# Four decoded weight units stay on chip through the later groups' first layers; five coded buffers instead of nine

## The chip, the core and the metric

The kernel runs on one core of a Trainium2 chip. The core has TensorE (PE, matrix products), VectorE (DVE), ScalarE (ACT), GpSimd (POOL) and SyncE (SP), which here only issues loads and stores; 16 DMA engines move the data. Every engine works through its own queue in order and waits on semaphores of the others. The metric is the device time of one execution in microseconds (us), the median of several runs.

## What is computed

Attention with 2 batches, 8 heads, 576 positions and a head size of 64, then an ELU-like layer of 512 to 2048 to 512, then a mixture of four experts of 512 to 1024 to 512, weighted by normalised probabilities:

```python
scores = scale * np.matmul(q, k.transpose(0, 1, 3, 2))
bias = -(cum[:, :, :, None] - cum[:, :, None, :])        # cum: running sum of max(s, 0)
scores = np.where(causal, -1e9, scores + np.minimum(bias, 0.0))
attn = np.exp(scores - scores.max(-1, keepdims=True))
attn = attn / (attn.sum(-1, keepdims=True) + 1e-09)
x = np.matmul(attn, v)                                   # as (1152, 512)
h = x @ w_in
g = np.where(h > 0.0, h, np.exp(np.minimum(h, 0.0)) - 1.0)
x = g @ w_out
p = domain_probs / (domain_probs.sum(-1, keepdims=True) + 1e-09)
for e in range(4):
    out += p[:, e:e + 1] * (np.maximum(x @ w1[e], 0.0) @ w2[e])
```

## The kernel before

**Tokens and units.** The 1152 tokens are worked in three groups of 256, 448 and 448. The first layer's weights are cut into 16 units (0 to 15) of 128 hidden columns with their 128 rows of w_out, 512 KB each; the experts' into 32 more (units 16 to 47). Group 0 runs its first layer (matmuls "up", L717, and "acc", L704) and then the experts (L614, as three matmuls of high and low halves). Group 1 and 2 run their first layers with L614 as well, and share the experts' layer behind that. The attention of the positions that group 0 doesn't need runs as a background to all this, one small step between two matmuls.

**Coded units.** For group 0 the 16 units come coded, two halves of 512 KB per unit, 32 halves in all, loaded by SP (L131). `decode_halves` turns a half into fp32: ACT takes the magnitude (L150) and the low bits (L157, into z), DVE puts them together (L158, L160). A decoded pair of units lies in a tile "wu" of a ring of five. When a unit is complete, POOL writes it to w_dec in DRAM (L163). In groups 1 and 2 `fetch` (L97, SP) reads each unit back from w_dec into a tile "raw" (ring of three), and `prepare` splits it into a high half (ACT, L103) and a low half (DVE, L87) in a "wu" tile. Units 16 and on are fetched by the same L97 from in_w.

**Where halves wait.** The coded halves of the first lap lie in tiles that are not needed yet: 2 in a wu tile, 3 in gt tiles, 9 in "cd" tiles made for them, then 11 in yh, yl, raw, xa and ox; the second lap takes yh, yl, raw and xa again. A half is loaded when the one that had its place is decoded.

**What the background needs.** `load_small` (L422, L424) loads the first 128 positions into a tile pt (five loads), `load` (L444 to L462) the first two larger jobs (eight loads each). `split` makes qs (L478), kh (L479), qb (L481) and kl (L87) of one head and loads 2 KB of bias rows behind qb and kl (L476, L477, from rows_d). One head's block is then: two score matmuls (L490 on kh and qs, L492 on kl and qb), DVE's reduction (L527), ACT's exponential (L532), DVE's normalisation (L505 to L507), PE's transpose (L542), ACT's copy of it (L557), and PE's product with v (L569). Scores and transposes share two banks "att". A first layer up uses one of two banks "up": PE may write one again when ACT (L721, L724) and DVE (L725) have read it.

**What sets the order.** The program names its operations in a loop over units, and a scheduler then orders each engine's queue when the kernel is built. On the chip each queue is fixed; SP may have eight loads under way.

Of the kernel before, what the change touches and what calls it, by code (L numbers as in the profile page):

```python
# [8 lines left out]
F32 = mybir.dt.float32  # L9
# [10 lines left out]
NAB, NCD = DFF // 128, F // 128  # L20
NU = NAB + E * NCD
# [26 lines left out]

N_LOW = 4

N_WU, N_GT, N_CD = 1, 3, 9

@with_exitstack
def tile_kernel(ctx, tc, qT, kT, v, s, w64, w, probs, out):
# [12 lines left out]
    psum = ctx.enter_context(tc.tile_pool(name="ps", bufs=1, space=bass.MemoryType.PSUM))  # L67
    PE, DVE, ACT, POOL, SP = nc.tensor, nc.vector, nc.scalar, nc.gpsimd, nc.sync

    BASE = ("ident", "mask", "maskp", "zero", "cum", "cum_2", "cum_t0", "cum_t1",  # L70
            "xa", "ox", "pr")
    EDGE = ("cum_p0", "cum_p1", "sm", "prs")
    L1 = ("wu", "raw", "gt", "e", "yh", "yl", "z0", "z1", "xf")

    def sb(shape, tag, bufs, dtype=F32):
        p = (base if tag in BASE else edge if tag in EDGE else l1_pool if tag in L1
             else att_pool[0])
        return p.tile(shape, dtype, tag=tag, name=tag, bufs=bufs)
# [9 lines left out]


    w64 = w64.bitcast(I32)  # L90
    w_dec = tc.dram_tile([NAB, 128, 1024], F32, name="w_dec")
    n_units = NU + NAB * (len(GROUPS) - 1)
    fetched, units = {}, {}

    def fetch(n):
        fetched[n] = t = sb([128, 1024], "raw", 3)
        SP.dma_start(out=t, in_=w[n - NAB] if n < NU else w_dec[(n - NU) % NAB])  # L97

# [8 lines left out]
    order = [(0, 0)] + [h for n in range(NAB - 1) for h in ((n + 1, 0), (n, 1))] + [(NAB - 1, 1)]  # L107

    small = [("yh", 1, 1), ("yl", 1, 1)] + [("raw", 3, 1)] * 3 + [("xa", 1, 3), ("ox", 1, 3)]
    turn = [("wu", 5, 2)] * N_WU + [("gt", 3, 1)] * N_GT + [("cd", N_CD, 1)] * N_CD + small * 2  # L110
    places = [(tag, bufs, n, i) for tag, bufs, n in turn for i in range(n)]
    coded, freed_by, last_in = {}, [], {}
    for i, (tag, bufs, many, k) in enumerate(places):
# [21 lines left out]
    def decode_halves(upto):  # L135

        while n_decoded[0] < min(upto, len(order)):  # L140
            i = n_decoded[0]
            n, part = order[i]
            if part == 0:
                if n % 2 == 0:
                    pair = sb([128, 2, 1024], "wu", 5)
                    units[n], units[n + 1] = pair[:, 0], pair[:, 1]
            x, m = coded.pop(i), units[n][:, 512 * part:512 * part + 512]
            high, low, mi = x[:, :, 1], x[:, :, 0], m.bitcast(I32)
            tc.keep_in_program_order(
                ACT.activation(m, high.bitcast(F32), AF.Abs, scale=2.0 ** -112))  # L150
            z = sb([128, 512], f"z{i % 2}", 1, I32)
            if i < N_LOW:
                tc.keep_in_program_order(DVE.tensor_scalar(
                    z, low.bitcast(U32), 7.49 / 2 ** 32, None, op0=ALU.mult))
            else:
                tc.keep_in_program_order(
                    ACT.activation(z, low.bitcast(U32), AF.Copy, scale=7.49 / 2 ** 32))  # L157
            DVE.scalar_tensor_tensor(out=mi, in0=mi, scalar=3, in1=z,  # L158
                                     op0=ALU.logical_shift_left, op1=ALU.bitwise_or)
            DVE.scalar_tensor_tensor(out=mi, in0=high, scalar=-2 ** 31, in1=mi,  # L160
                                     op0=ALU.bitwise_and, op1=ALU.bitwise_or)
            if part:
                POOL.dma_start(out=w_dec[n], in_=units[n])  # L163
            n_decoded[0] += 1
            fetch_halves()


    ident = sb([128, 128], "ident", 1)
    make_identity(nc, ident)

    mask = sb([128, S], "mask", 1)
# [3 lines left out]
    maskp = sb([128, 64], "maskp", 1)  # L175
# [6 lines left out]
    zero = sb([64, 256], "zero", 1)  # L182
# [7 lines left out]
    cum = sb([B * H, S], "cum", 1)  # L190
# [579 lines left out]
    yh, yl = (sb([128, NCC, tok], t, 1, F32R) for t in ("yh", "yl"))  # L770
# [3 lines left out]
    pr = pr_first  # L774
# [316 lines left out]
```

## Time and profile before

| | |
|---|---|
| median of 3 runs | 712.02 us (711.47 to 712.31) |
| span of the profiled execution, first to last instruction | 710.54 us (its whole time is not listed apart; the median is 1.48 above this span) |
| PE busy | 695.7 us (98%), 3670 instructions |
| DVE busy | 561.8 us (79%) |
| ACT busy | 366.9 us (52%) |
| POOL busy | 17.7 us (2%) |
| moved by DMA | 97.00 MB |
| mean granted TensorE clock | 0.997 |

The page is one profiled execution. Times are from the start of its span. A row of a timeline merges neighbouring equal instructions; "[3.94 <-DVE gt L725]" is idle time of that engine before the row, and what ended it. PE's instructions overlap, so a batch of eight that starts every 1.73 us is listed with 1.89.

### The profile page before, as it was taken

How to read it: one execution, taken by the hardware profiler on the slowest of the kernel's cores; microseconds unless marked ns; L12 is line 12 of the kernel's file. 1: busy time of each engine (PE TensorE's matmuls, PEld its weight loads, DVE VectorE, ACT ScalarE, POOL GpSimd, SP SyncE). 2: the span in 40 equal slices, each digit the busy share in tenths (PEclk: the TensorE clock that was granted, in tenths of full speed). 3: DMA queues.
4: the chain of work that ended last, by engine and by line, in shares of the span. 5: the costliest groups of instructions: out<-in, count | busy, mean ns of one | idle time of the engine just before them, and what ended most of it. 6: DMA issues, size and time to landing. Idle time of an engine off the chain costs nothing.

```text
span 710.5 us, 10311 instructions
## 1 busy us (share of the span) xinstructions
PE 695.7 (98%) x3670; PEld 594.1 (84%) x3670; DVE 561.8 (79%) x1158; ACT 366.9 (52%) x765; POOL 17.7 (2%) x40
## 2 busy tenths in 40 slices
PE   8999899999999999999999999999999999999997
PEld 7787688887878887887899988888888888888886
DVE  7798679887868988875975469988888888888765
ACT  5897679676667777666754343322222233322320
POOL 5011000000000000000000000000000000000000
PEclk9999999999999999999999999999999999999999
DMA  8999965765674553523552000111111111111002
GB/s 301 410 391 380 318 204 179 226 206 171 185 222 149 173 174 94 161 98 102 226 178 89 1 1 0 60 60 59 60 60 59 60 60 59 60 60 59 1 0 105
DMA packets 40868, 97.00 MB, mean 137 GB/s; under 512 B 4096, under 2 KB 17616, under 8 KB 40816
## 3 DMA queue, kind: packets, MB, share of 16 engines
q1 hardware_dynamic: 38288, 87.67, 37.0%
q0 software_dynamic: 2528, 8.67, 3.0%
q8 instruction: 29, 0.48, 0.3%
q14 instruction: 23, 0.19, 0.1%
HBM read 85.32 MB, written 11.01 MB: 136 GB/s over the span
## 4 chain that ended last, share of the span: by engine, by line
PE 89%; ACT 6%; DVE 2%; DMA 2%; issue 1%; POOL 0%; ACTq 0%; DVEq 0%; POOLq 0%
PE acc L614 39%; PE up L614 17%; PE att L926 11%; PE up L926 8%; PE att L569 3%; PE att L542 3%; ACT z L157 2%; ACT wu L150 2%; DMA raw<-in_w 2%; PE att L497 1%; PE att L490 1%; PE att L492 1%; PE acc L704 1%; PE att L362 1%; PE up L717 1%
## 5 line engine op out<-in xcount | busy, mean ns | idle before, releaser
L614 PE MATMUL acc<-w,h 128*128 128x512 f32 x672 | 172.0, 392 | 0.0
L614 PEld LDWEIGHTS acc<-w,h 128*128 128x128 f32 x672 | 126.1, 188 | 23.0 <-ACT h L936 0.2
L87 DVE TENSOR_TENSOR wu<-raw,wu 128x1024 fp32r<-128x1024 f32 x64 | 78.0, 1220 | 18.7 <-ACT wu L103 18.2
L614 PE MATMUL acc<-gt,wu 128*128 128x448 f32 x384 | 87.8, 372 | 0.0
L671 DVE SCALAR_TENSOR_TENSOR ox<-acc,pr,ox 128x512 f32<-128x512 f32 x105 | 78.5, 748 | 11.4 <-PE acc L614 9.1
L936 ACT ACTIVATE h<-c 128x448 fp32r<-128x448 f32 x48 | 27.4, 573 | 111.2 <-DVE c L942 111.2
L614 PEld LDWEIGHTS acc<-gt,wu 128*128 128x128 f32 x384 | 70.1, 188 | 7.8 <-issue 2.6
L103 ACT ACTIVATE wu<-raw 128x1024 fp32r<-128x1024 f32 x64 | 67.5, 1055 | 16.7 <-PE acc L614 14.5
L926 PE MATMUL att<-S,top 128*128 128x448 f32 x288 | 66.3, 365 | 0.0
L926 PEld LDWEIGHTS att<-S,top 128*128 128x128 f32 x288 | 54.0, 188 | 6.7 <-issue 0.2
L614 PE MATMUL acc<-wu,gt 128*128 128x512 f32 x192 | 56.1, 408 | 0.0
L614 PE MATMUL up<-yh,wu 128*128 128x256 f32 x256 | 53.4, 289 | 0.0
L937 DVE SCALAR_TENSOR_TENSOR h<-c,h 128x448 fp32r<-128x448 f32 x48 | 29.8, 623 | 18.7 <-ACT h L936 18.7
L614 PEld LDWEIGHTS up<-yh,wu 128*128 128x128 f32 x256 | 41.7, 189 | 3.4 <-issue 1.5
L926 PE MATMUL up<-x2a,top 128*128 128x448 f32 x192 | 44.2, 366 | 0.0
L614 PE MATMUL up<-xa,wu 128*128 128x448 f32 x192 | 43.5, 371 | 0.0
L614 PE MATMUL up<-ox,wu 128*128 128x448 f32 x192 | 41.5, 366 | 0.8 <-DVE e L729 0.8
L721 ACT ACTIVATE e<-up 128x448 f32<-128x448 f32 (+1 forms) x48 | 23.5, 489 | 34.0 <-PE up L614 30.2
L532 ACT ACTIVATE p<-p,nm 128x384 f32<-128x384 f32 (+4 forms) x56 | 34.5, 617 | 12.3 <-DVE nm L527 11.9
L926 PEld LDWEIGHTS up<-x2a,top 128*128 128x128 f32 x192 | 35.9, 188 | 4.8 <-ACT p L951 0.6
L936 ACT ACTIVATE h<-up 128x448 fp32r<-128x448 f32 x16 | 8.8, 547 | 59.5 <-PE up L926 59.5
L614 PEld LDWEIGHTS up<-ox,wu 128*128 128x128 f32 x192 | 36.0, 188 | 4.0 <-DVE e L729 1.1
(193 smaller groups left out, 1223.8 us busy)
## 6 DMA issues: line engine op xcount, KB each, us to landing
raw<-in_w SPq DMA_DIRECT2D x38, 512.0 KB
raw<-w_dec SPq DMA_DIRECT2D x32, 512.0 KB
raw<-in_w SPq DMA_DIRECT2D x16, 1024.0 KB
w_dec<-wu POOLq DMA_DIRECT2D x16, 512.0 KB, 7.4
cd<-in_w SPq DMA_DIRECT2D x9, 512.0 KB
k<-in_kT SPq DMA_DIRECT2D x16, 288.0 KB
xa<-in_w SPq DMA_DIRECT2D x5, 512.0 KB
cbp<-cum_d SPq DMA_DIRECT2D x16, 144.0 KB
```

The lines of the kernel that those rows point to most:

```text
L87: DVE.tensor_tensor(out=lo, in0=x, in1=hi.bitcast(F32), op=ALU.subtract)
L103: ACT.activation(t[:, 0], x, AF.Copy)
L150: ACT.activation(m, high.bitcast(F32), AF.Abs, scale=2.0 ** -112))
L532: ACT.activation(p, p, AF.Exp, bias=nm, scale=-1.0, accum_out=sm)
L542: PE.transpose(pt[:cb[c + 1] - cb[c], m, :], p[:, cb[c]:cb[c + 1]], ident)
L569: PE.matmul(o[64 * j:64 * j + 64, qs:nq], job["v"][:n, c, 64 * j:64 * j + 64], job["pt"][:n, j, c, qs:nq], start=c == 0, stop=c == n_c - 1)
L614: PE.matmul(o, a[m], b[n], start=first and i == 0, stop=last and i == 2)
L671: DVE.scalar_tensor_tensor(out=o_sb, in0=o, scalar=pr[:, i, e:e + 1], in1=o_sb, op0=ALU.mult, op1=ALU.add)
L721: ACT.activation(e, o, AF.Exp)
L926: PE.matmul(bank, tops[q][:, m, op, cs], x[:, n, c], start=first and c + i == 0, stop=c == 1 and i == 2, skip_group_check=True)
L936: ACT.activation(h[:, 0, u, cs], c, AF.Relu)
L937: DVE.scalar_tensor_tensor(out=h[:, 1, u, cs], in0=c, scalar=0.0, in1=h[:, 0, u, cs].bitcast(F32), op0=ALU.max, op1=ALU.subtract)
```

## The change

Two tiles "wr" of one pair of units each (16 KB per partition) are added. The decoded units 12 to 15 go into them rather than into wu, stay there until both later groups have split them, and are neither written to w_dec nor read back: 4 writes and 8 reads of 512 KB each are gone. The wr tiles hold the first four coded halves before that. The cd tiles become five instead of nine, and the tags zero, cum, cum_2, z0 and z1 move to the pool that is closed when the background begins.

```diff
-N_WU, N_GT, N_CD = 1, 3, 9
+N_WR, N_WU, N_GT, N_CD = 2, 1, 3, 5
+N_KEPT = 2 * N_WR
...
-    BASE = ("ident", "mask", "maskp", "zero", "cum", "cum_2", "cum_t0", "cum_t1",
-            "xa", "ox", "pr")
+    BASE = ("ident", "mask", "maskp", "cum_t0", "cum_t1", "xa", "ox", "pr")
     EDGE = ("cum_p0", "cum_p1", "sm", "prs")
-    L1 = ("wu", "raw", "gt", "e", "yh", "yl", "z0", "z1", "xf")
+    L1 = ("wr", "wu", "raw", "gt", "e", "yh", "yl", "xf")
...
-    w_dec = tc.dram_tile([NAB, 128, 1024], F32, name="w_dec")
+    w_dec = tc.dram_tile([NAB - N_KEPT, 128, 1024], F32, name="w_dec")
     n_units = NU + NAB * (len(GROUPS) - 1)
-    fetched, units = {}, {}
+    fetched, units, kept = {}, {}, {}
 
     def fetch(n):
+        if n >= NU and (n - NU) % NAB in kept:
+            fetched[n] = kept[(n - NU) % NAB]
+            return
...
-    turn = [("wu", 5, 2)] * N_WU + [("gt", 3, 1)] * N_GT + [("cd", N_CD, 1)] * N_CD + small * 2
+    turn = [("wr", N_WR, 2)] * N_WR + [("wu", 5, 2)] * N_WU + [("gt", 3, 1)] * N_GT + [("cd", N_CD, 1)] * N_CD + small * 2
...
                 if n % 2 == 0:
-                    pair = sb([128, 2, 1024], "wu", 5)
+                    if n < NAB - N_KEPT:
+                        pair = sb([128, 2, 1024], "wu", 5)
+                    else:
+                        pair = sb([128, 2, 1024], "wr", N_WR)
+                        kept[n], kept[n + 1] = pair[:, 0], pair[:, 1]
                     units[n], units[n + 1] = pair[:, 0], pair[:, 1]
...
-            if part:
+            if part and n not in kept:
                 POOL.dma_start(out=w_dec[n], in_=units[n])
```

The scheduler's order changes with it, in group 0, at the passage from the first layer to the experts. Lines of the changed kernel stand 3 to 7 lower: L97 becomes L100, L103 L106, L157 L164, L478 to L481 L485 to L488, L490 and L492 L497 and L499, L542 L549, L614 L621, L717 L724, L721 and L724 L728 and L731.

ACT, the decodes of the last halves (raw, xa) and the exponentials of the last units; before:

```order
L157 ACTIVATE z_760<-raw 128x512
L481 ACTIVATE qb<-pt 64x128 x2
L478 ACTIVATE qs<-pt 128x128 x2
L721 ACTIVATE e<-up 128x256
L724 ACTIVATE e<-e 128x256
L150 ACTIVATE wu<-xa 128x512
L157 ACTIVATE z_779<-xa 128x512
L150 ACTIVATE wu<-xa 128x512
L157 ACTIVATE z_785<-xa 128x512
L103 ACTIVATE wu<-raw 128x1024
L721 ACTIVATE e<-up 128x256
```

and in the changed kernel:

```order
L164 ACTIVATE z_756<-raw 128x512
L728 ACTIVATE e<-up 128x256
L731 ACTIVATE e<-e 128x256
L157 ACTIVATE wr<-xa 128x512
L164 ACTIVATE z_775<-xa 128x512
L157 ACTIVATE wr<-xa 128x512
L164 ACTIVATE z_780<-xa 128x512
L106 ACTIVATE wu<-raw 128x1024
L728 ACTIVATE e<-up 128x256
L106 ACTIVATE wu<-raw 128x1024
L731 ACTIVATE e<-e 128x256
L106 ACTIVATE wu<-raw 128x1024
```

The splits of pt (qb, qs) moved behind the exponential of unit 11 (the first e here), the decodes of xa and three splits of raw tiles, which follow one another sooner.

SP, the loads behind the last coded halves (xa<-in_w); before:

```order
L131 DMA xa<-in_w 128x1024 x2
L422 DMA pt<-in_qT 64x8x128 x2
L422 DMA pt<-in_kT 64x8x128
L97 DMA raw<-in_w 128x1024
L422 DMA pt<-in_kT 64x8x128
L97 DMA raw<-in_w 128x1024
L424 DMA pt<-in_v 128x512
```

and in the changed kernel:

```order
L134 DMA xa<-in_w 128x1024 x2
L100 DMA raw<-in_w 128x1024 x3
L429 DMA pt<-in_qT 64x8x128 x2
L429 DMA pt<-in_kT 64x8x128 x2
L431 DMA pt<-in_v 128x512
```

Three raw tiles (units 16 to 18) are fetched ahead of pt. Unit 19 follows 16 job loads and two pairs of bias rows later (before, units 18 and 19 followed the job loads directly, and two pairs of bias rows stood far ahead, before the second lap's yh).

PE, from the first expert's accumulation (acc, after 24 and 36 up matmuls) on; before:

```order
L614 MATMUL acc_1147<-wu,gt 128x512 x3
L614 MATMUL acc_1148<-wu,gt 128x512 x3
L614 MATMUL acc_1147<-wu,gt 128x512 x3
L614 MATMUL acc_1148<-wu,gt 128x512 x3
L614 MATMUL up<-yh,wu 128x256
L614 MATMUL up<-yl,wu 128x256
L614 MATMUL up<-yh,wu 128x256 x2
L614 MATMUL up<-yl,wu 128x256
L492 MATMUL att<-kl,qb 128x128
```

and in the changed kernel:

```order
L621 MATMUL acc_1141<-wu,gt 128x512 x3
L621 MATMUL acc_1142<-wu,gt 128x512 x3
L499 MATMUL att<-kl,qb 128x128
L497 MATMUL att<-kh,qs 128x128
L499 MATMUL att<-kl,qb 128x128
L549 MATMUL att<-ident,p 128x128
L497 MATMUL att<-kh,qs 128x128
L499 MATMUL att<-kl,qb 128x128
L621 MATMUL up<-yh,wu 128x256
L621 MATMUL up<-yl,wu 128x256
L499 MATMUL att<-kl,qb 128x128
L621 MATMUL up<-yh,wu 128x256 x2
```

The L492 and L542 of the first heads, which stood among the last units' matmuls of the first layer, now stand in a row behind 18 acc matmuls; of the four first L490 there, two stay. The number of instructions on PE, ACT and DVE is the same; SP has 8 fewer loads, POOL 4 fewer writes. In groups 1 and 2 the order is the same but for the splits that read wr.

## Rows read from the trace of the kernel before

**Rows 1.** The page, busy time, share of the span and instructions of each engine

```profile
PE 695.7 (98%) x3670; PEld 594.1 (84%) x3670; DVE 561.8 (79%) x1158; ACT 366.9 (52%) x765; POOL 17.7 (2%) x40
```

**Rows 2.** Windows: length, PE, PEld, DVE, ACT, POOL busy, PE clock, DMA share, GB/s

```profile
200.00:250.00 50.00, 49.82 (x299) 42.10 (x298) 39.08 (x104) 33.90 (x79) 0.00 (x0) 1.00 0.58 182
```

**Rows 3.** Instructions on w_dec: count, ns min/median/max, first and last start

```profile
L97 SPq DMA_DIRECT2D raw<-w_dec x32: 319/333/1482, 198.0 to 383.8; - x32
L163 POOL DMA_DIRECT2D w_dec<-wu x16: 532/534/571, 27.1 to 79.7; - x16
```

**Rows 4.** PE's timeline from 66 to 97 us: start, us, engine, line, tiles

```profile
66.33 1.89 PE L717 MATMUL up<-xf,wu 128*128 128x256 f32 x8
68.05 1.89 PE L704 MATMUL acc<-gt,wu 128*128 128x256 f32 x8
73.88 2.80 PE L717 MATMUL up<-xf,wu 128*128 128x256 f32 x8 [3.94 <-DVE gt L725]
...
83.14 0.41 PE L490 MATMUL att<-kh,qs 128*128 128x128 f32 x1
83.39 0.27 PE L492 MATMUL att<-kl,qb 68*128 68x128 f32 x1
...
90.83 0.47 PE L614 MATMUL up<-yh,wu 128*128 128x256 f32 x1
...
93.89 2.91 PE L614 MATMUL acc<-wu,gt 128*128 128x512 f32 x12
96.64 0.28 PE L614 MATMUL up<-yh,wu 128*128 128x256 f32 x1
```

**Rows 5.** Windows of 4 us around the end of the first layer

```profile
64.00:68.00 4.00, 4.00 (x20) 3.54 (x19) 3.81 (x8) 2.43 (x5) 0.53 (x1) 1.00 1.03 395
...
72.00:76.00 4.00, 2.12 (x7) 1.80 (x8) 1.85 (x4) 3.42 (x8) 0.00 (x0) 0.87 1.06 336
76.00:80.00 4.00, 3.52 (x11) 2.57 (x10) 3.26 (x7) 3.47 (x8) 0.85 (x2) 0.71 1.06 284
```

**Rows 6.** ACT's timeline from 65 to 73 us

```profile
65.77 0.67 ACT L157 ACTIVATE z<-raw 128x512 int32<-128x512 uint32 x1
70.06 0.51 ACT L481 ACTIVATE qb<-pt 64x128 fp32r<-64x128 f32 x2 [3.63 <-DMA pt<-in_qT]
...
72.56 0.36 ACT L721 ACTIVATE e<-up 128x256 f32<-128x256 f32 x1
```

**Rows 7.** Timeline of all engines, one head's block, 86 to 89 us

```profile
86.20 0.27 PE L492 MATMUL att<-kl,qb 68*128 68x128 f32 x1
...
86.69 0.28 DVE L527 CUSTOM_DVE_ANT_0 p<-att,mask 128x128 f32<-128x128 f32 x1
...
88.21 0.27 PE L542 MATMUL att<-ident,p 128*128 128x128 f32 x1
...
88.52 0.28 ACT L557 ACTIVATE pt<-att 128x128 f32<-128x128 f32 x1 [0.52 <-PE att L542]
```

**Rows 8.** Timeline of all engines around unit 20's split, 101 to 106 us

```profile
101.12 1.06 ACT L103 ACTIVATE wu<-raw 128x1024 fp32r<-128x1024 f32 x1
...
102.20 0.25 SPq L477 DMA_DIRECT2D kl<-rows_d  x1
...
102.26 1.21 DVE L87 TENSOR_TENSOR wu<-raw,wu 128x1024 fp32r<-128x1024 f32 x1
...
103.90 0.50 PE L614 MATMUL up<-yh,wu 128*128 128x256 f32 x2
...
105.18 0.22 PE L492 MATMUL att<-kl,qb 68*128 68x128 f32 x1
```

**Rows 9.** Windows behind that: the stretch to 124 us and the next 4 us

```profile
107.00:124.00 17.00, 17.00 (x112) 14.43 (x111) 16.17 (x45) 16.67 (x40) 0.00 (x0) 1.00 0.60 176
124.00:128.00 4.00, 4.00 (x26) 3.02 (x27) 4.00 (x9) 1.50 (x3) 0.00 (x0) 1.00 0.58 194
```

## The prediction

> **What bounds the kernel now.** I read the page's busy shares first, then TensorE's waits, then stretches. TensorE (PE) is busy 695.7 of 710.54 us [rows 1]. So traffic alone is worth little: where the 32 re-reads of w_dec run (198.0 to 383.8 us), the DMA engines are at most 0.58 busy while PE is busy 49.82 of 50 us [rows 2, 3]. Eight reads fewer there shorten nothing that ends last. The same view prices the other half: w_dec writes run from 27.1 to 79.7 us, and the last four stand in the one place where PE does wait.
>
> That place is 66 to 84 us, the last units of group 0's first layer. An up batch and an acc batch of eight records each take 1.72 to 1.73 us (66.33 to 68.05). The acc batch of 68.05 should be followed at 69.78; instead PE stands still for 3.94 us, until VectorE (DVE) frees an up bank, and then runs at half clock [rows 4]. The granted clock is 0.87 in 72 to 76 us and 0.71 in 76 to 80 [rows 5]. Why DVE is late is seen on ScalarE (ACT): after the z of 65.77 it waits 3.63 us for pt<-in_qT at the head of its queue, and it does not come to the exponential that PE is waiting for before 72.56 [rows 6]. That load waits because w_dec writes share the DMA engines. So the hole is one of order, not of bytes: ready work stands behind a DMA.
>
> **The change, part by part.**
>
> *Bytes.* Eight reads of 512 KB in 198 to 384 us: worth 0, since PE's own work covers them: 49.82 of 50 us [rows 2]. Without that cover eight landings of 512 KB at 182 GB/s would cost up to 23 us.
>
> *Four w_dec writes* (the thirteenth to sixteenth) leave the POOL queue at 65 to 80 us. Worth nothing alone, but the loads on SP behind them land sooner.
>
> *Order of the last units.* In the changed kernel the exponential of unit 11 stands directly behind the last raw decode on ACT, ahead of any pt load. ACT reaches it at 65.77 + 0.57 = 66.3, six us sooner than 72.56. The 3.94 us hole and the half clock after it go. From 69.78 PE has eight batches left (up 13, acc 11, up 14, acc 12, up 15, acc 13, acc 14, acc 15) at 1.73 = 13.8 us, and two first score matmuls (kh, qs) at 0.25 (83.14 to 83.39 [rows 4]): 84.1 instead of 90.83. What could take its place: raw fetches of units 16 to 18 are now ahead of pt on SP, and ACT's splits of them (L103) stand among the exponentials. Raw tiles become free at the same decodes as now, the last of them soon after the z of 65.77 [rows 6]; with no w_dec write beside them I estimate three landings of 512 KB between 70 and 73, at the 336 to 395 GB/s of these windows [rows 5], and the pt loads until 76. ACT and DVE then hold PE for some 0.3 us before up 14. I take 84.3. So about 6.5 us are won by then.
>
> *What is late next.* The attention of the later groups, whose first blocks before ran in between the last units (83 to 90 us, hidden beside PE work), is now queued behind more layer 2 work. PE does 36 up matmuls rather than 24 (24 take 93.89 - 90.83 = 3.06 us, so 4.6), and 18 acc rather than 12 (2.75, so 4.1) [rows 4]: 84.3 + 8.7 = 93.0. There PE finds L492 of the first head, and everything behind it is a chain with little to cover it. One block from its L492 to its transpose is 88.21 - 86.20 = 2.0 us, through DVE, ACT and DVE again, and 0.31 more until ACT takes the transpose [rows 7]. Worked along the new queues, with these durations:
>
> First transpose at 93.0 + 2.3 (DVE does two heads in turn) = 95.3, its copy by ACT to 95.8. Only then stands unit 19's split on ACT: 0.95 us, 96.8. DVE's half, 1.15 us: 98.0. PE can use the second half of unit 19 then. DVE then does fifteen short steps of 0.15 to 0.36 us (reductions, normalisations, small splits; 3.6 us, all queued ahead of unit 20's split), ACT two exponentials, two copies and six splits of 0.2 meanwhile, with two short waits: ACT ends unit 20's split at 101.2, DVE at 102.8. Before, these two ended at 102.07 (101.12 + 0.95) and 103.4 [rows 8]. So of 6.5 us some 0.6 to 0.9 are left at that point. PE stood idle for about 6 of 10 us on the way; it is the same work, later on the engines that must do it first.
>
> *Why it stays so.* From 107 to 124 us ACT is busy 16.67 of 17 us and DVE 16.17 [rows 9]. Unit 20's second half was used by PE at 103.90, 0.5 us after DVE had it. PE, ACT and DVE are in step there, so an advance on PE cannot be carried past 100 us unless ACT and DVE have it too. After 124 ACT has slack (1.50 of 4), and PE alone sets the end; what it has then is kept.
>
> *Unknown: landing of the small rows.* Each block needs 2 KB into qb and kl (L476, L477), in the new order issued only after the block two before has been read. The trace gives no landing. From one issue at 102.20 to its unwaited use at 105.18 it is at most 2.98 us [rows 8]; the other bound is 0. At 0 nothing is gained over my sum, since ACT holds PE at those places; at 2.98 four blocks slip, and DVE's unit 20 with them, by 1.2 us. I take 2.0, below the bound, because that use had not waited. The Trainium skill (DMA: Bandwidth & Descriptors, section "Anatomy of one DMA") puts the fixed cost of a DMA near 2.0 us; by that the sum would be the same.
>
> *Clock.* A gap of 3.94 us was followed by half clock here. The new stretch has PE mostly idle from 93 to 96 and about half idle until 103, so I expect one half-clock stretch like the one of rows 5 in it ((0.13 + 0.29) of 4 us, over 0.5, is 3.4 us). It doubles PE's share of the chain only: it costs between 0 (hidden in waits) and 1.7 us (half of it, all PE); I take 0.3, since PE is not what the chain waits for.
>
> *Pools, buffers.* The tags zero, cum, z0, z1 move between pools; before the small turns there are 4 halves in wr, 2 in wu, 3 in gt and 5 in cd, against 2, 3 and 9, so the first lap holds 25 halves either way and the decodes until 65 us keep their times: 0. The first splits reuse wu buffers whose w_dec write is older: 0.
>
> Sum: -0.8 + 0.3 = -0.5 us, 711.5. The profiled execution's span is 710.54 and the median of the runs 712.02, 1.5 us of which lie outside it and stay; I set the sum against the median, since the runs differ by 0.84 among themselves.
>
> **The rivals.**
>
> *The gain is kept* (faster). If ACT and DVE never idle from 93 on, DVE's queued work up to the end of unit 20's split is two splits of 1.15 and some 26 short steps of about 0.22 [rows 7, 8], 8 us: done at 101.0 rather than 103.4, -2.4, or 709.6. For it: before, DVE and ACT did the same blocks with idle time between. Against it: each block's transpose, copy and split are in one line on three engines, and the unit's split stands behind the copy in ACT's own queue. In the extreme that attention did not hold PE at all, the 6.5 us would all be kept: 705.5; I give that only a few per cent, since rows 9 show the engines full.
>
> *The chain costs more than the hole did* (slower). The place is 93 to 103 us. If the half clock lasts through two stretches there, each at up to 1.7 us, or rows land at 2.98 us, or pt lands two us later than I put it (then the chain starts two later), the second half of unit 20 comes after 103.4 + 1.4, and PE, with no slack from 124 on, gives it to the end: 713.5 to 715. It decides from 1.9 us more than my sum. For it: PE is idle there as never before in this kernel. Against it: PE's own share of the chain is small. On the clock the Trainium skill (TensorE: Matmul & The Clock Gate, section "HAM oscillation — how this bites in real kernels") states that idle gaps in a loop bring the half rate back again and again; by that rule alone the time would be the 713.5 to 715 given here. The trace agrees for one gap [rows 4, 5], and shows no stretch of many short ones.
>
> *The change doesn't do what it says*: the order is fixed when the kernel is built, so ACT cannot fall back behind pt; only if raw 16 landed after 73 would its split take the pt load's role as the plug in front of an exponential. Half of the hole would stay (3 us), and with it the chain starts later: 714.
>
> **How the numbers follow.** The likeliest: near 711.5 (710.6 to 713.4, within 0.2%, 1.4 us, which is about what a measurement of this kernel can tell from no change): 0.57. Gain kept in part or whole: 0.22. More expensive chain, or a plug again: 0.21. The range 709.4 to 714.2 leaves one in ten on either side.
>
> **What would show it.** Right: no wait of PE on L725's gt near 70 us, the clock 1.00 there; layer 2's first up matmul near 84.3; PE idle 5 to 7 us between 93 and 103, released by DVE's p and wu and ACT's wu; ACT and DVE full from 102 on; unit 20's second half on PE near 103. Wrong: PE idle under 3 us there (then faster), or a PE clock below 0.8 for more than 4 us or row loads named as its releasers (then slower), or any difference after 130 us.

## The result, and the profile of the changed kernel

The changed kernel took 721.27 us (median of 4 runs, 720.5 to 721.61), the kernel before 712.12 us beside it (711.47 to 712.31): 1.0121 times as long [1.0106 to 1.0137], 9.15 us slower. The profiled execution has a span of 719.7 us at a mean granted clock of 0.988, against 710.5 at 0.997.

The page of the changed kernel, its line of busy times as in [rows 1]:

```profile
PE 700.5 (97%) x3670; PEld 598.8 (83%) x3670; DVE 562.5 (78%) x1158; ACT 367.8 (51%) x765; POOL 15.6 (2%) x36
```

The instructions are as many as before, and PE is busy 4.8 us longer with the same ones: the clock was lower for part of the time. From 158 us on, matching steps stand 9.9 to 9.2 us apart in the two traces, and behind 130 us PE has no wait over 0.8 us in either. So the 9 us are lost before, and PE's timeline shows three places (columns as in [rows 4]):

```profile
36.17 3.78 PE L724 MATMUL up<-xf,wu 128*128 128x256 f32 x8 [5.63 <-DVE gt L732]
39.75 2.22 PE L711 MATMUL acc<-gt,wu 128*128 128x256 f32 x8
...
72.88 1.89 PE L724 MATMUL up<-xf,wr 128*128 128x256 f32 x8
...
84.56 0.33 PE L497 MATMUL att<-kh,qs 128*128 128x128 f32 x1 [1.16 <-ACT kh L486]
...
91.61 0.47 PE L621 MATMUL up<-yh,wu 128*128 128x256 f32 x1
...
96.28 4.27 PE L621 MATMUL acc<-wu,gt 128*128 128x512 f32 x18
100.39 0.22 PE L499 MATMUL att<-kl,qb 68*128 68x128 f32 x1
...
102.38 0.33 PE L549 MATMUL att<-ident,p 128*128 128x128 f32 x1 [0.94 <-DVE p L514]
...
104.02 0.39 PE L621 MATMUL up<-yh,wu 128*128 128x256 f32 x1 [0.51 <-ACT wu L106]
...
105.28 0.80 PE L621 MATMUL up<-yh,wu 128*128 128x256 f32 x2 [0.70 <-DVE wu L87]
...
111.63 0.80 PE L621 MATMUL up<-yh,wu 128*128 128x256 f32 x2
```

*At 36 us* PE waits 5.63 us for gt, a result of DVE, in a place for which the prediction had no term. Unit 12's up batch then starts at 72.88, not at 66.33 [rows 4], 6.55 us late. *At 70 us* the hole of the kernel before is gone, as predicted, and only 1.16 us of waiting for kh at 84.56 stands in its place: layer 2 starts at 91.61, against 90.83, so some 5.8 of the 6.55 us were taken back. *From 100.39 us* comes the row of attention steps; unit 20's second half follows at 111.63 instead of 103.90 [rows 8]: 7.7 us late, and behind it PE is busy nearly all the time, so the loss stays.

Windows of the changed kernel (columns as in [rows 2]) show the clock at the first and third place:

```profile
32.00:36.00 4.00, 0.00 (x0) 0.00 (x0) 3.74 (x7) 3.92 (x8) 1.05 (x2) 0.70 1.03 390
36.00:40.00 4.00, 3.83 (x9) 3.11 (x10) 2.25 (x5) 0.01 (x1) 0.54 (x2) 0.50 1.02 405
...
102.00:106.00 4.00, 2.05 (x9) 1.58 (x10) 3.19 (x13) 3.08 (x11) 0.00 (x0) 0.91 0.43 136
106.00:110.00 4.00, 3.95 (x19) 3.21 (x18) 2.46 (x14) 2.94 (x10) 0.00 (x0) 0.50 0.44 132
110.00:114.00 4.00, 3.74 (x20) 3.22 (x20) 3.84 (x14) 3.13 (x12) 0.00 (x0) 0.50 0.63 198
114.00:118.00 4.00, 4.00 (x23) 3.39 (x23) 2.61 (x8) 3.46 (x9) 0.00 (x0) 0.81 0.42 123
```

From 105.3 to 115.5 us the clock is at its lower level, 1.2 GHz: the shortfalls of these four windows (0.09, 0.50, 0.50 and 0.19 of 4 us each, over 0.5) make 10.2 us. In the kernel before every window of 4 us from 80 to 128 us has 1.00 (rows 9 show those from 107 us on). The early hole has such a stretch too: the shortfalls of 32 to 40 us (0.30 and 0.50) and 0.05 in the window behind make 6.8 us, so the loss at this place is a wait and slow matmuls behind it (3.78 us for a batch that takes 1.89 elsewhere).

What the early hole waits for stands in the timelines of ACT and DVE in the changed kernel:

```profile
29.27 0.42 ACT L731 ACTIVATE e<-e 128x256 f32<-128x256 f32 x1
...
34.49 0.69 DVE L167 SCALAR_TENSOR_TENSOR wu<-gt,wu 128x512 int32<-128x512 int32 x1
35.10 0.68 DVE L165 SCALAR_TENSOR_TENSOR wu<-wu,z 128x512 int32<-128x512 int32 x1
35.70 0.42 DVE L732 SCALAR_TENSOR_TENSOR gt<-up,e 128x256 f32<-128x256 f32 x1
```

and of the kernel before:

```profile
26.08 0.69 DVE L160 SCALAR_TENSOR_TENSOR wu<-gt,wu 128x512 int32<-128x512 int32 x1
...
29.26 0.42 ACT L724 ACTIVATE e<-e 128x256 f32<-128x256 f32 x1
...
29.71 0.42 DVE L725 SCALAR_TENSOR_TENSOR gt<-up,e 128x256 f32<-128x256 f32 x1
```

The first gt result of the layer needs a gt tile, and a gt tile holds a coded half until that half is decoded. Its exponential was ready on ACT at 29.7 in both kernels. Before, the halves lay in wu (0, 1) and then gt (2 to 4), so the first gt tile was free after the third decode, at 26.8, and DVE wrote the result at 29.71, as soon as the exponential was there. Now they lie in wr (0 to 3), wu (4, 5) and then gt (6 to 8): the tile is free after the seventh decode, at 35.2, and the result comes at 35.70. The `turn` line of the diff says so.

### The profile page after: what moved, and what is told of

It reads as the page before. It is cut to its first block, busy times and chain, and to the rows that moved or that the text cites. A ratio compares the mean times of both kernels' runs of the same rounds, so it can differ in the third digit from the quotient of the medians.

```text
span 719.7 us, 10283 instructions
## 1 busy us (share of the span) xinstructions
PE 700.5 (97%) x3670; PEld 598.8 (83%) x3670; DVE 562.5 (78%) x1158; ACT 367.8 (51%) x765; POOL 15.6 (2%) x36
## 4 chain that ended last, share of the span: by engine, by line
PE 85%; issue 8%; DMA 2%; POOL 2%; DVE 1%; ACT 1%; SPq 0%; POOLq 0%; DVEq 0%; ACTq 0%
PE acc L621 39%; PE up L621 17%; PE att L933 11%; PE up L933 8%; PE att L576 3%; PE att L549 3%; PE att L504 1%; PE att L497 1%; DMA pt<-in_kT 1%; PE att L499 1%; DMA w_dec<-wu 1%; POOL w_dec L170 1%; PE acc L711 1%; DVE wu L87 0%; ACT wu L106 0%
## 5 line engine op out<-in xcount | busy, mean ns | idle before, releaser
L621 PE MATMUL acc<-w,h 128*128 128x512 f32 x672 | 172.0, 392 | 0.0
L621 PEld LDWEIGHTS acc<-w,h 128*128 128x128 f32 x672 | 126.1, 188 | 23.0 <-ACT h L943 0.2
L621 PE MATMUL acc<-gt,wu 128*128 128x448 f32 x384 | 87.8, 372 | 0.0
L87 DVE TENSOR_TENSOR wu<-raw,wu 128x1024 fp32r<-128x1024 f32 x56 | 68.4, 1221 | 16.6 <-ACT wu L106 16.1
L621 PEld LDWEIGHTS acc<-gt,wu 128*128 128x128 f32 x384 | 70.1, 188 | 7.8 <-issue 2.6
L106 ACT ACTIVATE wu<-raw 128x1024 fp32r<-128x1024 f32 x56 | 59.0, 1053 | 17.3 <-PE acc L621 13.8
L621 PE MATMUL up<-yh,wu 128*128 128x256 f32 x256 | 55.7, 299 | 1.3 <-DVE wu L87 0.7
L621 PE MATMUL acc<-wu,gt 128*128 128x512 f32 x192 | 56.1, 409 | 0.0
L621 PEld LDWEIGHTS up<-yh,wu 128*128 128x128 f32 x256 | 43.8, 198 | 4.6 <-issue 1.5
L621 PE MATMUL up<-xa,wu 128*128 128x448 f32 x192 | 43.6, 371 | 0.0
L728 ACT ACTIVATE e<-up 128x448 f32<-128x448 f32 (+1 forms) x48 | 23.4, 488 | 37.5 <-PE up L621 30.8
L621 PE MATMUL up<-ox,wu 128*128 128x448 f32 x192 | 41.5, 366 | 0.8 <-DVE e L736 0.8
L621 PEld LDWEIGHTS up<-ox,wu 128*128 128x128 f32 x192 | 36.0, 188 | 4.0 <-DVE e L736 1.1
```

What stands on the lines that cost most here:

```text
L87: DVE.tensor_tensor(out=lo, in0=x, in1=hi.bitcast(F32), op=ALU.subtract)
L106: ACT.activation(t[:, 0], x, AF.Copy)
L621: PE.matmul(o, a[m], b[n], start=first and i == 0, stop=last and i == 2)
L728: ACT.activation(e, o, AF.Exp)
```

## The experiments

Two causes stood to be told apart first: the early hole and the row of steps. Theory A was that both cost, B that the row costs all (the late hole would have absorbed the early one), C that the early hole costs all. Behind that came why the row costs what it does, and why the hole at 70 us gave so little. Each kernel's ratio is to the kernel before as timed beside it (medians of 712.47 to 713.04 us). Differences between two changed kernels are of their medians; where these were timed beside different runs of the kernel before, they carry its drift, up to 0.9 us (712.12 beside the changed kernel, 713.04 beside e3).

### Early hole or row of steps: e1, e2, e4

e1 is the changed kernel with the halves in another order:

```diff
-turn = [("wr", N_WR, 2)] * N_WR + [("wu", 5, 2)] * N_WU + [("gt", 3, 1)] * N_GT + ...
+turn = [("gt", 3, 1)] * N_GT + [("wr", N_WR, 2)] * N_WR + [("wu", 5, 2)] * N_WU + ...
```

> The changed kernel with one list turned round: the gt tiles take the first three coded halves again (as nearly before, where they took the third to fifth), the wr tiles the next four, wu two, cd five. Theory A (two causes: gt tiles that hold late halves stop DVE's first evictions and open a hole of 5.63 us on PE near 30 us; the row of attention steps behind the experts' first units costs the rest): the hole near 30 us goes, PE reaches the first lone L499 near 93.5 us, 6.5 to 7 earlier than 100.39, and the end follows: 713.5 to 715. Theory B (the row of attention steps alone costs the 9 us, and the early hole would have been taken back by the later one near 70 us): 719 to 721. Theory C (the early hole alone): 711 to 712, as the prediction had it.

Measured: 715.62 us (712.37 to 719.31, 10 runs), 1.0044 [1.0023, 1.0065]. The early hole is gone (0.82 us at 38.66, as before) and 5.65 of the 9.15 us with it (6.1, if each kernel is set against the kernel before beside it: 9.15 less 3.04). That is the outcome of theory A, 0.6 us above its range. The row of steps is as in the changed kernel, 5.15 us earlier, with its half clock; windows of e1:

```profile
96.00:100.00 4.00, 1.62 (x8) 1.01 (x8) 2.86 (x12) 3.43 (x13) 0.00 (x0) 0.98 0.42 133
100.00:104.00 4.00, 3.87 (x18) 3.32 (x18) 2.77 (x16) 2.58 (x9) 0.00 (x0) 0.50 0.49 135
104.00:108.00 4.00, 3.69 (x18) 2.98 (x18) 3.50 (x16) 3.74 (x14) 0.00 (x0) 0.50 0.44 132
108.00:112.00 4.00, 4.00 (x23) 3.68 (x22) 3.40 (x10) 2.97 (x10) 0.00 (x0) 0.74 0.53 145
```

The ten runs fall into two sets by their mean granted clock: 0.997 in those of 712.37, 713.14 and 713.68 us, 0.986 to 0.993 in the other seven (714.42 to 719.31).

e2 puts the late gt alone into the kernel before:

```diff
-turn = [("wu", 5, 2)] * N_WU + [("gt", 3, 1)] * N_GT + [("cd", N_CD, 1)] * N_CD + ...
+turn = [("cd", N_CD, 1)] * 4 + [("wu", 5, 2)] * N_WU + [("gt", 3, 1)] * N_GT + [("cd", N_CD, 1)] * 5 + ...
```

> The kernel before with one list changed: four cd tiles take the first four coded halves, then wu two, gt three, cd five, so gt holds the seventh to ninth half as in the changed kernel; nothing is kept on chip, and the attention steps stand among the last units as before. The hole near 30 us of 5 to 6 us should appear on PE. Theory A and B: the later hole near 70 us, which a load sets and not PE, then gets smaller by about as much, so 712 to 714. If the early hole adds in full: 718 to 719.

Measured: 719.71 us (718.25 to 721.36), 1.0102 [1.0082, 1.0121]. PE's waits in e2:

```profile
36.27 3.78 PE L717 MATMUL up<-xf,wu 128*128 128x256 f32 x8 [5.64 <-DVE gt L725]
78.30 3.15 PE L717 MATMUL up<-xf,wu 128*128 128x256 f32 x8 [4.70 <-DVE gt L725]
```

Both holes stand side by side: the later one does not absorb the early one, and what I had expected of that fell. Taken out of the changed kernel the early hole is worth 5.65 us, put into the one before 7.1: both places cost, as A says, and B and C fall (C also by the 3.0 us that are left in e1).

e4 is the kernel before with nothing but the pool of z0 and z1 changed:

```diff
-    L1 = ("wu", "raw", "gt", "e", "yh", "yl", "z0", "z1", "xf")
+    L1 = ("wu", "raw", "gt", "e", "yh", "yl", "xf")
```

> The kernel before with one edit: the tags z0 and z1 move to the pool that is closed when the background begins, and no more (zero and cum stay, nothing is kept, nine cd tiles). In the built program this alone gives PE the row of attention steps behind 36 up and 18 acc matmuls. gt is early, so no hole near 30 us. Theory A: the hole near 70 us goes (6 us won) and the row gives it back with its half clock: 712.5 to 715. Theory B: 719 to 721. Theory C and the prediction: 711 to 712.

Measured: 720.73 us (718.85 to 721.55), 1.0107 [1.0089, 1.0124]. This line alone gives PE the order of the changed kernel, 36 up, 18 acc, then the row (the line "up<-yh" is layer 2's first up matmul):

```profile
83.83 0.47 PE L490 MATMUL att<-kh,qs 128*128 128x128 f32 x1 [3.73 <-ACT kh L479]
...
93.47 0.47 PE L614 MATMUL up<-yh,wu 128*128 128x256 f32 x1
...
97.97 4.27 PE L614 MATMUL acc<-wu,gt 128*128 128x512 f32 x18
```

So the kept units are not needed to reorder the passage: moving two scratch tiles (2 KB per partition each) to that pool, done in order to make room, is enough. z0 and z1 live until the last decode; why the scheduler then places the first heads' blocks later is not shown by a run.

The time missed what A gave for e4 (712.5 to 715) and lies in B's range; B falls by e1 and e2 alone. A had counted the hole near 70 us as won, and in e4 it is not: PE waits 1.52 us at 75.94 and 3.73 at 83.83, the clock is at its lower level for some 6.8 us around and behind that (0.90, 0.50 and 0.75 in 80 to 92), and layer 2 starts at 93.47, 2.6 us later than in the kernel before. So e4's 8.15 us are not the price of the row alone.

### What the bytes are worth: e3, e7, e5

e3 is e1 with the four writes put back (`if part:` in front of the POOL write); nobody reads them.

> The kernel of e1 (gt tiles first, four units kept) with the four w_dec writes of units 12 to 15 put back. Nobody reads them; the order on PE, ACT, DVE and SP is that of e1 row for row. This asks what the four writes are worth by themselves. The prediction said nothing alone, only loads on SP that land sooner. Theory W (the writes take DMA time from the loads at 66 to 84 us, 2 MB at 395 GB/s = 5.3 us): against e1, raw 16 to 18 and pt land some 5 us later, layer 2's first up near 90 us instead of 86.6, time e1 + 4 to 5 us = 720 to 721, which is what e4 (old weights, new row) took. Rival N (nothing): time within 1 us of e1's 715.6, layer 2 at 86.6. If e4's 720.7 came from something else than the writes, e3 will be near e1.

Measured: 719.65 us (718.37 to 722.05), 1.0104 [1.0085, 1.0123]: 4.0 us over e1 (3.6, each against the kernel before beside it). PE's timeline of e3, and behind it the same two places of e1:

```profile
81.95 0.33 PE L497 MATMUL att<-kh,qs 128*128 128x128 f32 x1 [2.89 <-ACT kh L486]
...
88.56 0.47 PE L621 MATMUL up<-yh,wu 128*128 128x256 f32 x1
```

```profile
80.03 0.33 PE L497 MATMUL att<-kh,qs 128*128 128x128 f32 x1 [1.35 <-ACT kh L486]
...
86.64 0.47 PE L621 MATMUL up<-yh,wu 128*128 128x256 f32 x1
```

pt lands later, kh with it, and layer 2 starts 1.9 us later. The two traces end 3.4 us apart (717.8 and 714.4); the other 1.5 us come behind layer 2's start, where the stretch at 1.2 GHz lasts some 13.7 us in e3's windows (0.57, 0.50, 0.50, 0.72 from 100 to 116), 10.2 in e1's. Four writes that were to be worth nothing alone are worth about 4 us in this kernel. The Trainium skill (DMA: Bandwidth & Descriptors, section "Queues, rings and completion order") says that each DMA engine takes turns between its queues, packet by packet; by that the POOL writes take their share from SP's loads however the loads are ordered, and e3 agrees: SP issued pt<-in_kT at 70.27 and ACT had it at 81.58, against 70.64 and 79.66 in e1.

e7 is e3 with the eight reads put back as well (`fetch` without its first three lines).

> e3 with the eight reads put back as well: units 12 to 15 are decoded into the wr tiles, written to w_dec, and in both later groups fetched into raw tiles and split from there, as in the kernel before. This asks what the eight reads are worth by themselves. The prediction: 0, since PE is busy 49.8 of 50 us there; then e7 is within 0.7 us of e3. Rival: up to 23 us if nothing covered them; any loss would show as PE waits between 198 and 384 us. PE's waits there should stay below 1 us in all.

Measured: 719.35 us (718.93 to 722.36), 1.0105 [1.0088, 1.0122], as e3. PE's waits between 198 and 392 us are the same two (0.8 and 0.2 us) in both. The reads are worth nothing, as predicted.

e5 keeps two units instead of four, so that z0 and z1 can stay where they were: `N_WR, N_CD = 1, 7`, gt first, z0 and z1 in L1. PE's order at the passage is then that of the kernel before.

> The changed kernel with gt first, one wr tile (units 14 and 15 kept), seven cd tiles, and z0 and z1 back in their old pool: two writes and four reads of 512 KB are gone, and the attention steps stand among the last units as before. If only places and order matter: 711 to 712.5, as before, with the hole near 70 us still there. If the traffic itself is worth something (two writes of 512 KB that stood beside the pt loads): down to 708.

Measured: 712.62 us (712.03 to 715.66), 1.0007 [0.9994, 1.0019]. Old order, old hole:

```profile
74.27 3.29 PE L724 MATMUL up<-xf,wu 128*128 128x256 f32 x8 [4.33 <-DVE gt L732]
```

Two writes fewer bring nothing while the exponential stands behind the pt load.

### The clock by itself: e6, e11

e6 is e1 with 16 matmuls more, whose results are not used, each behind a score product or a batch of transposes of the row:

```diff
+                last = PE.matmul(pss[:, :e - a], job[j, "qb"][:, qs], job[j, "kl"][:, a:e],
+                                 start=False, stop=True)
+                warm(last, 8)
...
+        def warm(after, n):
+            if g == 1 and n_warm[0] < 2 * n:
+                n_warm[0] += 1
+                with tc.issue_after(after.ins):
+                    PE.matmul(ps("acc2", 1)[:, :256], ident, mask[:, :256], start=True, stop=True)
...
+            warm(last, 8)
```

> e1 with 16 matmuls more (ident by 256 columns of mask, into an idle bank, their result unused), one behind each of the first score products and each batch of transposes of the later groups, in the row of attention steps. The rest of the row keeps its order up to the 7th up matmul behind it, later steps move a little. Theory K (e1's 3.5 us above the kernel before, and its spread of 712.4 to 719.3, are the half clock behind the row): the clock stays 1.00 from 91 to 110 us, time 712 to 713.5 and spread below 2 us; the dummies lie in PE's waits. Rival D (the chain through DVE and ACT costs it, the clock is a consequence): the clock is up but the time stays 715 to 717, or rises by the dummies' own time, 16 by 0.2 to 0.45 = 3 to 7 us, where they are in the way.

Measured: 716.75 us (715.8 to 719.45), 1.0066 [1.0049, 1.0083]. The clock is 1.00 from 92 to 132 us, but PE is full from 100 us on, and ten of the sixteen stand there. Two windows and the group of the dummies (two records each):

```profile
96.00:100.00 4.00, 3.33 (x14) 2.00 (x14) 3.19 (x13) 2.81 (x11) 0.00 (x0) 1.00 0.44 136
100.00:104.00 4.00, 4.00 (x28) 3.27 (x26) 3.63 (x15) 3.06 (x12) 0.00 (x0) 1.00 0.54 140
```

```profile
L514 PE MATMUL acc<-mask,ident 128*128 128x256 f32 x32 | 10.3, 405 | 0.0
```

The time lies in rival D's range, but this did not tell the theories apart: what the clock may have given, the dummies took of PE's own time. So e11 keeps only the first six, which lie where PE waits (`warm(last, 3)`).

> e6 with 6 dummy matmuls rather than 16: only the first six, which lie where PE waits in the row of attention steps (92 to 99 us); the ten that stood in e6 where PE had work are gone. In e6 a dummy took 0.5 us of PE and the clock was 1.00 throughout; ten by 0.5 is 5 us. Theory K (e1's excess is the half clock behind the row): clock 0.997 or more, 711.5 to 713.5. Rival D: 715 to 717, as e1, with half clock behind 100 us again or with waits in its place.

Measured: 712.88 us (711.82 to 717.5, 13 runs), 1.0002 [0.9994, 1.0011], with a mean clock of 0.996 or more in twelve of the runs. The one at 717.5 and 0.992 is the profiled one: in it raw 17 landed late (ACT waits 3.78 us for it at 75.60), PE stood 3.62 us at 80.68, and the half clock behind that is at 80 to 87 us; in the row itself, from 99.38 on, the clock was 1.00:

```profile
90.78 0.47 PE L631 MATMUL up<-yh,wu 128*128 128x256 f32 x1
```

```profile
100.00:104.00 4.00, 3.16 (x15) 1.90 (x14) 2.85 (x12) 3.27 (x12) 0.00 (x0) 1.00 0.38 121
104.00:108.00 4.00, 4.00 (x24) 2.88 (x24) 3.66 (x16) 3.06 (x11) 0.00 (x0) 1.00 0.45 147
```

Six useless matmuls in PE's idle time are worth 2.7 us (715.62 to 712.88). The traces agree, late load or not: from layer 2's first up matmul to the end e11 takes 715.5 - 90.78 = 624.7 us, e1 714.4 - 86.64 = 627.8. Behind the first seven up matmuls of the row the order of e11 differs a little from that of e1; but e1's own three runs with a mean clock of 0.997, all in e1's order, took 712.37 to 713.68 as well.

### The hole at 70 us: order or bytes? e8 to e10, e12 to e15

The prediction called the hole one of order. These kernels keep PE's old order and move only what stands in ACT's queue ahead of the exponentials. e8 is e5 with the pt loads allowed sooner and the first split behind an exponential.

> The kernel of e5 (two units kept, z0 and z1 left where they were, old passage on PE) with two edits: the five loads of pt may be issued only behind the third-last coded half instead of the last, and the first two splits of pt (qb, qs) only behind the last exponential of unit 11 that is already named. ACT then meets the exponential that PE waits for before it waits for pt. Theory: the hole of 4.3 us near 74 us and the half clock behind it go without the row of attention steps, unit 20's second half 3 to 6 us sooner than before, time 707 to 710. Rival (in step anyway): ACT and DVE are full from 107 to 124 us and give the gain back, 711 to 712.5. Rival (plug elsewhere): the pt loads, sooner in SP's queue, delay the last coded halves or raw 16 by 2 to 3 us and PE waits for these instead: 712 to 715.

Measured: 712.42 us (711.13 to 713.41), 0.9996 [0.9986, 1.0006]. One split (qb) stayed ahead of the exponentials, now earlier; ACT's timeline of e8:

```profile
65.17 0.31 ACT L488 ACTIVATE qb<-pt 64x128 fp32r<-64x128 f32 x1 [4.67 <-DMA pt<-in_qT]
```

The hole moved from 74 to 66 us (3.40 us on PE), and nothing was gained. e9 is the kernel before with both splits gated:

```diff
-            split(items[0])
...
+        def sp():
+            with tc.issue_after(last_e[-1].ins) if g == 1 else nullcontext():
+                split(items[0])
...
+        parts = [start, sp] if g == 1 else [start, lambda: split(items[0])]
...
+                            with tc.issue_after(last_e[-1].ins) if g == 1 and n < 1 else nullcontext():
+                                split(items[n + 1])
```

> The kernel before with one edit: the splits of pt for the first two heads may be issued on ACT only behind the exponential of the last unit named by then. ACT's queue becomes that of the changed kernel at this place (exponentials of units 11 and on, then the splits); PE's queue stays that of before, with the first heads' scores among the last units' matmuls; all 16 units are still written and read. This asks what step 2 of the prediction (the 3.94 us hole behind the pt load) is worth by itself. Theory P (the prediction's own): the hole and the half clock at 72 to 80 us go, 6.5 us by layer 2's first up, of which ACT and DVE, full from 107 us, give all but 0.6 to 2.4 back: 710 to 712. Theory T: the hole is one of traffic (4 writes, 3 raw fetches and pt share the DMA engines), PE then waits as long at kh or at raw 16's split: same time as before within 1 us, wait of 3 to 4 us moved to 78 to 84 us, as the 3.73 us wait of e4.

Measured: 714.35 us (713.91 to 715.17), 1.0027 [1.0017, 1.0037], slower. ACT's exponential of unit 11 no longer waits, but that of unit 12 stands behind the split of raw 16 (the raw tile of unit 16). ACT and PE in e9:

```profile
76.99 1.06 ACT L103 ACTIVATE wu<-raw 128x1024 fp32r<-128x1024 f32 x1 [6.53 <-DMA raw<-in_w]
```

```profile
80.30 3.40 PE L721 MATMUL up<-xf,wu 128*128 128x256 f32 x8 [5.84 <-DVE gt L729]
```

SP issued that load at 66.47, behind three of the five pt loads, and ACT had it at 76.99. e10, the same edit on e5 (two writes fewer):

> e5 (two units kept, old passage on PE) with the same edit of ACT's order as e9. Two writes fewer than e9 between 66 and 84 us. Theory P: hole gone, 709 to 711. Theory T: each of the two writes saved is worth 1.2 us of the wait that is left, so 1 to 2.5 us under e9, 709.5 to 711.5; the waits left sit at kh or at a split of raw. Rival: same as e9 within 0.7 us, since ACT and DVE full from 107 us take it back.

Measured: 715.82 us (714.45 to 716.34), 1.0040 [1.0027, 1.0052]: the same wait (6.78 us) at the same place; fewer writes did not help here. e12 (on e9) and e13 (on e10) also gate the splits of units 16 and 17:

```diff
-            prepare(prepare_at[0])
+            with tc.issue_after(last_e[-1].ins) if prepare_at[0] in (16, 17) else nullcontext():
+                prepare(prepare_at[0])
```

> e9 (the kernel before, splits of pt behind the exponentials) with a second edit of ACT's order alone: the splits of units 16 and 17 (raw tiles) also go behind the exponentials of units 12 and 13. In e9 the exponential of unit 12 stood behind the split of unit 16, whose raw tile landed only near 77 us, and PE waited 5.84 us. Now ACT holds nothing that waits for a load ahead of the exponentials of units 11, 12 and 13. PE's order stays the old passage, 16 units are written and read. Theory O (the hole of the kernel before is one of order on ACT, as step 2 said): layer 2's first up at 85 to 87 us instead of 90.83, no half clock from 66 to 86; of these 4 to 5 us what ACT and DVE, full from 107 to 124 us, do not take back: 708 to 711. Theory T (traffic): PE waits at kh or at unit 16's high half instead, 712 to 714.

> e10 (two units kept) with the second edit of e12. Theory O: as e12, 708 to 711. If the two writes saved are worth 1.2 us each where PE waits for loads, and e12 still shows waits between 76 and 90 us, 1 to 2 us under e12; if e12 shows none there, the same as e12.

Measured: e12 716.04 us (714.48 to 718.36), 1.0048 [1.0032, 1.0065]; e13 712.73 us (711.97 to 716.43), 1.0009 [0.9994, 1.0024]. All exponentials of these units were free now, and PE ran from 38.6 to 78.6 us without a wait. Then, DVE and PE in e12:

```profile
85.14 0.49 DVE L239 TENSOR_SCALAR bias<-cbp,cum_p 128x512 f32<-128x512 f32 x1 [5.19 <-DMA cbp<-cum_d]
```

```profile
86.61 0.47 PE L490 MATMUL att<-kh,qs 128*128 128x128 f32 x1 [4.97 <-ACT kh L479]
```

The next instruction that needs a load (the bias of the first larger job, on DVE) holds the reduction of the first scores; ACT stands 4.43 us for it, at an exponential that is queued ahead of the next kh. In e13 the same wait is 4.13 us on DVE and 3.84 on PE. e14 (on e13) and e15 (on e12) issue the second larger job's eight loads later (`load(jobs[1])` moved from `start` into the fifth background step).

> e13 (two units kept, all splits gated) with the eight loads of the second larger job issued two background steps of four later, behind raw 18 and 19 rather than ahead of them. In e13 PE waited 3.84 us for kh, since DVE stood 4.13 us at the bias of the first larger job for its cbp load, one of some 20 loads that share the DMA engines between 66 and 88 us. Theory T (bytes between 66 and 90 us set the passage): some 0.8 MB fewer there, 2 us at 395 GB/s: the wait shrinks to 1 to 2 us, 710 to 712. Theory O (order of the instructions alone): the same wait of 3 to 4 us, 712 to 714. PE's order changes behind it (the first heads' transposes and v products stand earlier), which can cost or give 1 to 2 us of its own.

> The same later loads on e12 (the kernel before with all splits gated, 16 units written and read), which waited 4.97 us for kh behind DVE's 5.19 us wait for cbp. Theory T: the wait shrinks by about 2 us, to some 3 us, and two writes more than e14 cost 1 to 2.5 us: 711.5 to 714. Theory O: as e12, 715 to 717.

Measured: e14 714.90 us (714.38 to 716.28), 1.0030 [1.0019, 1.0041]; e15 716.82 us (716.19 to 718.15), 1.0054 [1.0040, 1.0067]. The wait is not shorter (4.35 and 5.80 us on PE): the loads that I moved stand behind cbp on SP, so what sets cbp's landing should be ahead of it, which no run shows. PE's order moved with them, so these two say nothing finer. That fewer bytes ahead of it would help is indicated by e12 against e13 (3.3 us for two writes) and e15 against e14 (1.9 us), and contradicted by e9 against e10 (1.5 us the other way, with the longer half clock in e10). What a hole at this passage costs if no load is late was not reached: no kernel here is without one. Of the seven forecasts only those for e8 (its two rivals) and e15 (theory O) have the measured time in a stated range, so neither theory, order or traffic, was priced by these runs. None of the fifteen kernels is shown to be faster than the kernel before (the lowest ratio is 0.9996 [0.9986, 1.0006], e8).

## Why the prediction was wrong, step by step

**Pools and buffers** (taken at 0): this step failed, twice. I counted the places of the first lap, 25 halves either way, and not whose places they are. The gt tiles are the one place that PE's own first units wait for, and they went from the third to the seventh decode: 5.65 us (e1), 7.1 us in the kernel before (e2). And the move of z0 and z1, listed with the same zero, is what reorders the passage (e4: 720.73 against 712.58 beside it, 8.15 us). I had described that reordering in full and had not asked which edit makes it.

**Eight reads** (0): right; e7 and e3 agree within the spread of their runs (719.35 and 719.65).

**Four writes** ("worth nothing alone, but the loads on SP behind them land sooner"): the first half is wrong for the kernel as changed: 4.0 us (e3 against e1). The mechanism was named (the loads behind them land sooner), but priced at nothing. In e5, where ACT's plug stands first, two of them were indeed worth nothing.

**Order of the last units** (6.5 us, layer 2 at 84.3): the hole went and the clock stayed at 1.00 there. Without the early hole, layer 2 starts at 86.64 (e1), 4.2 us sooner than before and not 6.5: raw tiles and kh held PE 0.26, 0.35 and 1.35 us, where 0.3 was taken. The prediction put the late pt load down to the writes; but in e5, with two writes fewer, the hole is no smaller (4.33 us against 3.94). That the hole is "one of order, not of bytes" does not hold: e9, e10, e12 and e13 each removed one plug by order and met the next load. In e3, with the changed order and all 16 writes, layer 2 starts at 88.56, 2.3 us sooner than before (some attention steps moved behind that point), and without the four writes 1.9 us sooner still (e1): between these two kernels and the one before, order and bytes have about equal parts.

**What is late next** (the row: from the first L492 2.3 us to the first transpose, 5.0 to unit 19's second half, 9.8 until unit 20 is split on DVE): the first terms hold. In the changed kernel the transpose is at 102.38 - 100.39 = 2.0, unit 19's second half at 105.28 - 100.39 = 4.9. Unit 20's second half is at 11.24, where 9.8 and a little was due: 1.2 to 1.4 us more, all of it behind the fall of the clock. In these 11.24 us PE is busy 8.03, at a mean clock of 0.72: it stands idle 3.2 us, not the 5 to 7 of the prediction's signs, since its own steps took longer.

**Clock** (0 to 1.7, taken 0.3, one stretch of 3.4 us): mis-sized. The stretch is 10.2 us and costs 2.7 us (e1 against e11). Its bound rested on PE's share of the chain up to unit 20 alone; the half clock went on for another 4 us, where PE, ACT and DVE are in step. The prediction's own sign for "slower", a clock below 0.8 for more than 4 us, is what came. The second half-clock stretch, 6.8 us around the early hole, belongs to a place that the prediction had at 0. The rival that the chain costs more named this mechanism, with up to two stretches and 713.5 to 715; e1 took 715.62. The Trainium skill (TensorE: Matmul & The Clock Gate, section "A second HAM failure mode: psum-queue depth-cycling") tells of a kernel whose clock oscillates because PE idles briefly and often between groups of matmuls; the row agrees as far as the short waits go, with none listed over 0.94 us; the clock fell once there and rose once.

**Rows of 2 KB** (landing 2.0, bounds 0 to 2.98): no wait of PE, ACT or DVE in the row names them, and no run shows their landing. The section of the Trainium skill that the prediction cites there (DMA: Bandwidth & Descriptors, "Anatomy of one DMA") is on DMAs that GpSimd issues; these rows are loaded by SP.

**The sum again, from the runs**: row of steps with all 16 units written +6.6 (e3), four writes fewer -4.0 (e1 against e3), halves in the changed order +5.65 (the change against e1): +8.3. This adds the same medians in and out and comes to the changed kernel less the 713.04 beside e3, so it splits the loss but does not test the split; the 0.9 us to 9.15 is the drift of the kernel before. Single edits of the kernel before do test it: +7.1 (e2) and +8.15 (e4), less 4.0 for the writes, make 11.3, 2.1 too many. The causes do not simply add, and each price holds for the kernel in which it was measured.

The prediction's own sum, -0.5, is near what e1 comes to when the clock is held (e11: +0.4, six dummies included), but partly by luck. Layer 2 starts 2.3 us later in e1 than the prediction had it; with its chain taken as it stands that would have made +1.8. So the chain was right in its first terms; why its later ones cost some 1.4 us less than forecast once the clock is held is not shown by a run.

## What to carry to other kernels

When buffers serve a second purpose, write down for each tile when its first proper user needs it, and give it the earliest turn; the count of places says nothing. A wait removed by order where the DMA engines are busy all the time (a share of 0.96 to 1.13 in the windows of 4 us from 28 to 92 us) is likely to come back at the next instruction that needs a load, on whichever engine: look for that instruction before counting a gain. And a row of short dependent steps with PE half idle should be priced with the lower clock for the whole row and what follows it, or filled with PE work from elsewhere.

## What the runs showed of the hardware

The clock fell without any long gap: in the changed kernel no wait of PE in the row is over 0.94 us, and yet it was at 1.2 GHz for 10.2 us, while a 1.16 us wait at 84.56 among full stretches left it at 1.00. With six matmuls more, listed with some 0.65 us each, it stayed up in a row in which PE was still idle 0.84 of 4 us (100 to 104 in e11). In the kernel before PE stood still from 69.94 to 73.88 and the clock was still at 1.00 in 72 to 74 us; it fell only behind that (0.73 in 74 to 76, 0.50 in 76 to 78). And how much of the time it is down differs between executions of one kernel: e1's ten runs lie 6.9 us apart, at mean clocks of 0.986 to 0.997. Only one of them (716.36 us, 0.993) has a trace, so what set off the longer stretches in the others is open; in e11's run of 717.5 us it was a late load.
